# Moving the regroupings of k and q behind the additions to ut, in a fused sigmoid-attention and MLP-mixer kernel

## The chip, the cores and the metric

The kernel runs on one core of one Trainium2 chip. The metric is the device time of one execution in microseconds, and the number quoted for a kernel is the median of its timed executions. Besides those there is one profiled execution, whose trace gives each engine's instructions in order of time. Engines are named as the profile names them: PE is the matrix engine (PEld its weight loads), DVE the vector engine, ACT the scalar engine, POOL the GpSimd engine, SP the engine that here only issues DMAs.

## The reference

Inputs q, k and v have the shape (8 batches, 12 heads, 448 positions, 64). Attention without a softmax is followed by a mixer over positions (token part) and over channels (channel part):

```
scores = q @ k^T / 8 - log(448);  x = sigmoid(scores) @ v     # x: (8, 448, 768)
h  = relu(x^T @ w_tok1) @ w_tok2;  u  = x + h^T               # 448 -> 256 -> 448
h2 = relu(u @ w_ch1) @ w_ch2;      out = u + h2               # 768 -> 1536 -> 768
```

## The kernel before, in words

**Cycles.** The work runs in 24 cycles, three per batch: batch b, unit u (0, 1, 2), cycle c = 3b + u. A unit is four of the twelve heads. The instruction order of every engine is written out by hand; nothing is scheduled by a planner, and each engine executes its own list in order. In cycle c, PE computes the scores of (b, u) in seven pieces (`qk`, L184), between them the attention output of the unit before (`av`, tile `xa`, L211), the token part of the unit two cycles back (`tok_tail`, `tok1`, tile `tk`, then `ytrans`, tile `yt`, L312), and pieces of the channel part of an earlier batch (`c` tiles; L367 and L605 are the second channel product, L491 the first one, done once per batch behind the third cycle in the function `sevens`, in a scheme with seven block products).

**What DVE does in a cycle.** It casts `xa` out of PSUM (`xT`, L220, with a small copy L226), adds the token part to it (`ut`, L319, "the additions to ut"), adds and moves out the channel results (`o`, L564, L571, L757), and regroups the loaded k and q (L126): `raw_k` and `raw_q` hold a batch as it was loaded, `rel_k` and `rel_q` the same with pairs of heads side by side. Three regroupings, one per unit, make one tensor of one batch.

**PSUM banks.** `xa`, `tk` and `yt` of batches from the third on take turns in banks 0 and 1: the next user on PE waits until DVE or ACT has read the one before. So PE's `xa` of a cycle waits for the additions to ut of the cycle before, and PE's `tk` waits for the casts `xT`.

**SP's queue.** SP issues, in order, the DMA transposes of k and q of the coming batch (`tr_k`, `tr_q`, L139, 21 blocks of 128x128 each), of the attention output (`xn`, L236, 8 blocks), of the sum u (`un`, L326, 24 blocks), and the stores of the results (L577, L766). A transpose of k or q is issued when its three regroupings are done. `tr_k` and `tr_q` of a batch are read by the first `qk` of that batch.

**POOL's queue.** After the opening, POOL only issues loads. `gated_loads(b)` first copies two columns of `tr_q` of batch b+1 (L971, "the gate"), so that it waits for that transpose, and then issues the loads of v of batch b+1 and of k and q of batch b+2, each in two halves. There is one buffer for the loaded k and one for q, and two for v.

**Where the regroupings stand.** `through_dma(b, 0)` is the list of eight pieces "regroup k three times, transpose k, regroup q three times, transpose q":

```
for t in ("k", "q"):
    for u in range(u0, NU):
        pieces.append(lambda t=t, u=u: relayout(b, t, u))
    pieces.append(lambda t=t: dma_transpose(b, t, u0))
```

Cycles 6 to 8 (third batch) hand the pieces for the fourth batch out one at a time between pieces of channel work (`work`), and `sevens` takes up to two that are left. Cycles 9 to 23 call `some(n)` at two places: n = `within` after the third `qk`, n = `behind` at the end of the cycle, ahead of `ytrans`.

Of the kernel before, what the change touches and what calls it, by code (L numbers as in the profile page):

```python
# [23 lines left out]
NU = 3  # L24
# [6 lines left out]
def kernel(  # L31
# [13 lines left out]
    B, H, S, E = q.shape  # L45
# [39 lines left out]
    def bank(shape, dtype, name):  # L85

        if opening_banks:
            n = opening_banks.pop(0)
        else:
            n = at_bank[0]  # L90
            at_bank[0] = (n + 1) % 4
        return pp.tile(shape, dtype, tag=f"m{n}", bufs=1, name=name)
# [7 lines left out]
    def raw_tile(b, t):  # L100
        if (b, t) not in raw:
            tag, bufs = f"raw_{t}", 2 if t == "v" else 1
            if b == 1 and t != "v":
                tag = f"rel_{t}"
            raw[b, t] = pa.tile(
                [128, NU, 2, NJ, E], FP16, tag=tag, bufs=bufs, name=f"raw_{t}_{b}"
            )
        return raw[b, t]

    def load(b, t, src, u0, u1):  # L110

        for g in range(2):
            dst = raw_tile(b, t)[64 * g : 64 * g + 64, u0:u1, :, :, :]
            heads = src[b, 6 * g + 2 * u0 : 6 * g + 2 * u1]
            nc.gpsimd.dma_start(
                out=dst.rearrange("p u hi j e -> p (u hi) (j e)"),
                in_=heads.rearrange("h (p j) e -> p h (j e)", j=NJ),
            )

    def relayout(b, t, u):  # L120

        if (b, t) not in rel:
            rel[b, t] = pa.tile(
                [128, NU, NJ, 2, E], FP16, tag=f"rel_{t}", bufs=1, name=f"rel_{t}_{b}"
            )
        nc.vector.tensor_copy(  # L126
            out=rel[b, t][:, u, :, :, :],
            in_=raw[b, t][:, u, :, :, :].rearrange("p hi j e -> p j hi e"),
        )
# [8 lines left out]
    def dma_transpose(b, t, u0, u1=NU):  # L138
        nc.sync.dma_start_transpose(  # L139
            out=tr_tile(b, t)[:, u0:u1, :, :].rearrange("e u j r -> e (u j) r"),  # L140
            in_=rel[b, t][:, u0:u1, :, :, :].rearrange("r u j hi e -> r (u j hi e)"),
        )

    def through_dma(b, u0):

        pieces = []
# [4 lines that stand above are left out]
        return pieces  # L151

    def by_unit(b, u0):

        pieces = []
# [4 lines that stand above are left out]
                pieces.append(lambda t=t, u=u: dma_transpose(b, t, u, u + 1))  # L160
        return pieces
# [143 lines left out]
    def ytrans(b, u, banks=()):  # L305
        for g in range(2):
            db = NU * g + u
            if banks:
                at_bank[0] = banks[g]
            ps = bank([128, 512], FP32, f"yt_{b}_{db}")  # L310
            for tcb in range(2):
                nc.tensor.matmul(  # L312
                    out=ps[:, 0:S],
                    lhsT=h1[b, u][:, tcb, g, :],
                    rhs=w2[:, tcb, :, :],
                    start=(tcb == 0),
                    stop=(tcb == 1),
                )
            nc.vector.tensor_tensor(  # L319
                out=uts[b % 2][:, db, 0:S], in0=xTs[b % 2][:, u, g, 0:S], in1=ps[:, 0:S], op=ADD  # L320
            )
# [531 lines left out]
    def pieces_ch2(b, groups):  # L853
        for t, half in groups:
            for n in range(0, NCB, 3):
                yield 3 * DH, lambda t=t, half=half, n=n: ch2(b, t, half, n, n + 3)

    def pieces_last(b):
        for n in range(0, NCB, 3):
            yield 3 * DH, lambda n=n: ch2_last(b, n, n + 3)  # L860
# [108 lines left out]
    def gated_loads(b):  # L969

        nc.gpsimd.tensor_copy(  # L971
            out=gate[:, :], in_=tr[b + 1, "q"][:, NU - 1, NJ - 1, 126:128]
        )
        if b > 1:
            load(b + 1, "v", v, 0, NU)
        for t, src in (("k", k), ("q", q)):
            if b + 2 < B:
                load(b + 2, t, src, 0, NU)

    ON_DMA = range(N_FIRST, N_CYCLES)  # L980

# [3 lines left out]
    for c, cb in ((N_FIRST, 3), (N_FIRST + 1, 8)):  # L985
        b, u = divmod(c, NU)
        before = divmod(c - 1, NU)
        ahead = divmod(c + 1, NU)
        copies = []
# [27 lines left out]
        if u == 2:  # L1017
            copies = by_unit(2, 1)
# [33 lines left out]
    pending, copies = [], []  # L1052
    early = weight_sums()
    lane = [0]
    for c in range(2 * NU, ONE_RUN):
        b, u = divmod(c, NU)
        before, ahead = divmod(c - 1, NU), divmod(c - 2, NU)


        if c == 2 * NU:  # L1060
            first = c
            pending, shares = [*pieces_ch2(0, by_half[2:]), *pieces_last(0)], [10, 10, 10]
            total = sum(w for w, f in pending)
            spent = 0

        def work(share):
            goal = 3 * sum(shares[: c - first]) + share * shares[c - first]
            done = 0
            while pending and spent + done < total * goal / 90:
                w, f = pending.pop(0)  # L1070
                if len(pending) % 4 == 3:
                    lane[0] ^= 1
                at_bank[0] = 2 + lane[0]
                f()
                done += w
                if copies:
                    copies.pop(0)()
                elif early:
                    early.pop(0)()
            return done  # L1080

        qk(b, u, 0)
        qk(b, u, 1)
        at_bank[0] = 0
        av(*before)
        xtrans_dma(*before)
        qk(b, u, 2)
        if c == 2 * NU + 2:
            copies += through_dma(3, 0)[NU + 1 :]
        spent += work(1)  # L1090
        qk(b, u, 3)
        qk(b, u, 4)
        at_bank[0] = 0
        tok_tail(*ahead)
        tok1(*ahead, with_scores=True)
        if c == 2 * NU + 1:
            copies = through_dma(3, 0)[: NU + 1]
        spent += work(2)
        if c == 2 * NU + 2:
            utrans(b - 1)  # L1100
            token_sums(b - 1)
        qk(b, u, 5)
        qk(b, u, 6)
        if u < 2:
            at_bank[0] = 0
            ytrans(*ahead)
        spent += work(3)
        if u == 2:
            sevens(b - 1)
            at_bank[0] = 0  # L1110
            ytrans(*ahead)
            gated_loads(b)
    assert not copies and not pending and not early

    def some(n):
        for f in copies[:n]:
            f()
        del copies[:n]

    for c in range(ONE_RUN, N_CYCLES):  # L1120
        b, u = divmod(c, NU)
        before, ahead = divmod(c - 1, NU), divmod(c - 2, NU)
        if b == NU:
            within, behind = ((0, 0), (4, 2), (2, 0))[u]
        else:
            within, behind = 2, 2
        if u == 0:
            assert not copies
            copies += through_dma(b + 1, 0) if b + 1 < B else output_sums()

        X, Y = 2, 0
        at_bank[0] = X
        turn0, turn1, rest = ch2_pair(b - 2, u)
        part = len(turn1) * 2 // 3
        qk(b, u, 0)
        qk(b, u, 1)
        for f in turn0:
            f()  # L1140
        qk(b, u, 2)
        some(within)
        if c == ONE_RUN + 2:
            gated_loads(b)
        if u == 2:
            utrans(b - 1)
        at_bank[0] = Y
        av(*before, 0, 4)
        qk(b, u, 3)
        av(*before, 4, NJ)  # L1150
        xtrans_dma(*before)
        if u == 2:
            token_sums(b - 1)
        qk(b, u, 4)
        for f in turn1[:part]:
            f()
        qk(b, u, 5)
        for f in turn1[part:]:
            f()
        at_bank[0] = Y  # L1160
        tok_tail(*ahead)
        qk(b, u, 6)
        tok1(*ahead, with_scores=True)
        rest()
        some(behind)
        if u == 1 and NU < b < B - 1:
            gated_loads(b)
        if u == 2:
            at_bank[0] = Y + 1
            for w, f in pieces_last(b - 2):  # L1170
                f()
            sevens(b - 1)
        at_bank[0] = Y
        ytrans(*ahead)
    assert not copies


# [5 lines left out]
    def halves(b, t, half):  # L1183
        return [lambda n=n: ch2(b, t, half, n, n + 6) for n in (0, 6)]

    first, second = halves(lot, 2, 0), halves(lot, 2, 1)
# [33 lines left out]
    first, second = halves(B - 1, 2, 0), halves(B - 1, 2, 1)  # L1220
# [47 lines left out]
```

## Time and profile before

| | us |
|---|---|
| median of three timed executions | 348.65 (347.54, 348.65, 351.4) |
| the profiled execution, its own time | 347.11 |
| its span, from the first to the last instruction | 345.3 |
| PE busy | 338.2 (98%) |
| DVE busy | 213.7 (62%) |
| ACT busy | 210.9 (61%) |
| POOL busy | 56.7 (16%) |
| three regroupings of a tensor (L126, about 0.61 each) | 1.67 to 1.8 |

The busy time of PE is modelled from pipelined matrix products, so that a short wait inside a run of products shows as a longer run, and not as idle time. In the lines of the timeline, the first number is the start in us from the span's beginning, the second the length, and the brackets behind a line tell how long the engine sat idle before it and what ended that. The DMA of a transpose or a load goes on after the issuing engine is done with it; the trace gives the time "to landing" apart.

### The profile page before, as it was taken

The page shows a single profiled execution, that of the slowest core. Times are in us where ns is not written, and L with a number is a line of the kernel's source. Part 1 is how long each engine was busy: PE and PEld are TensorE (multiplying, and loading weights), DVE is VectorE, ACT ScalarE, POOL GpSimd, SP SyncE. Part 2 cuts the span into 40 slices and gives each one's busy share as a digit, 9 for nine tenths or more (in the row PEclk, how much of TensorE's full clock was granted, in tenths as well). Part 3 has the DMA queues.
Part 4 walks back from the last instruction along what each step waited for, and adds up shares of the span by engine and source line. Part 5 has one row for each costly group of instructions (what it writes and reads, how often), then busy time and mean ns, then how long its engine had stood idle before and what let it go on. Part 6 is the DMA issues. An engine that isn't in the chain of part 4 may idle for free.

```text
span 345.3 us, 10256 instructions
## 1 busy us (share of the span) xinstructions
PE 338.2 (98%) x4465; PEld 241.5 (70%) x4465; DVE 213.7 (62%) x427; ACT 210.9 (61%) x271; POOL 56.7 (16%) x98
## 2 busy tenths in 40 slices
PE   7999999999999999999999999999999999999994
PEld 4555556555886679766896669766896779767962
DVE  2377466577775665756575654765665684976662
ACT  3996846487748865788448865688448875111400
POOL 8982440230040013000400013000100000000000
PEclk9999999999999999999999999999999999999999
DMA  7999999999999999989997999979963592035406
GB/s 120 174 170 189 208 203 203 169 175 219 200 181 205 198 184 208 153 126 164 181 228 87 165 193 156 199 108 170 176 135 30 82 171 68 1 78 128 79 2 159
DMA packets 104380, 52.17 MB, mean 151 GB/s; under 512 B 76432, under 2 KB 101264, under 8 KB 104336
## 3 DMA queue, kind: packets, MB, share of 16 engines
q1 hardware_dynamic: 78944, 29.70, 49.2%
q0 software_dynamic: 25168, 21.50, 41.5%
q8 instruction: 35, 0.57, 0.7%
q10 hardware_dynamic: 224, 0.33, 0.4%
q14 instruction: 9, 0.07, 0.1%
HBM read 43.45 MB, written 11.01 MB: 158 GB/s over the span
## 4 chain that ended last, share of the span: by engine, by line
PE 88%; ACT 4%; DMA 3%; DVE 2%; issue 1%; POOL 0%; DVEq 0%; ACTq 0%
PE c_ab L491 14%; PE c L367 12%; PE qk L184 9%; PE c_c L491 8%; PE xa L211 8%; PE c L605 6%; PE tk L289 5%; PE c L734 5%; PE yt L312 5%; PE c L541 4%; ACT att L191 4%; PE c L695 4%; PE c L344 3%; DMA raw_k<-in_k_dram 2%; DMA first_q<-in_q_dram 1%; PE c_b L491 1%
## 5 line engine op out<-in xcount | busy, mean ns | idle before, releaser
L191 ACT ACTIVATE att<-qk,att_bias 128x896 f16<-128x896 f32 x168 | 155.3, 1015 | 34.0 <-PE qk L184 33.7
L184 PE MATMUL qk<-tr_q,tr_k 64*64 64x448 f16 x672 | 59.5, 359 | 0.3 <-ACT att L191 0.2
L491 PEld LDWEIGHTS <-c 128*128 128x128 f16 x504 | 47.8, 98 | 1.9 <-issue 1.8
L367 PE MATMUL c<-c,h 64*64 64x384 f16 x960 | 47.1, 322 | 0.0
L220 DVE CAST xT<-xa 128x448 f16<-128x448 f32 x48 | 27.7, 620 | 31.1 <-PE xa L211 31.0
L211 PE MATMUL xa<-att,raw_v 64*64 64x448 f16 x672 | 40.3, 349 | 0.1
L512 ACT ACTIVATE pt_ab<-c_ab 128x896 f32<-128x896 f32 x21 | 19.3, 917 | 30.8 <-PE c_ab L491 30.8
L367 PEld LDWEIGHTS <-h 64*64 64x64 f16 x960 | 29.5, 107 | 11.0
L491 PEld LDWEIGHTS <-sum 128*128 128x128 f16 x378 | 36.3, 98 | 0.0
L184 PEld LDWEIGHTS <-tr_k 64*64 64x64 f16 x672 | 21.5, 105 | 19.2 <-issue 11.9
L564 DVE TENSOR_TENSOR o<-un,c 128x384 f32<-128x384 f16 x34 | 18.8, 554 | 23.9 <-PE c L605 20.6
L319 DVE TENSOR_TENSOR ut<-xT,yt 128x448 f16<-128x448 f16 x48 | 27.5, 614 | 2.5 <-PE yt L312 2.5
L211 PEld LDWEIGHTS <-raw_v 64*64 64x64 f16 x672 | 21.5, 107 | 10.6 <-issue 1.0
L971 POOL COPY gate<-tr_q 128x2 f16<-128x2 f16 x6 | 1.1, 184 | 153.0 <-DMA tr_q<-rel_q 153.0
L303 ACT ACTIVATE h<-tk 128x256 f16<-128x256 f32 x42 | 14.3, 412 | 14.8 <-PE tk L289 14.8
L541 PE MATMUL c<-c,h 128*128 128x384 f16 x120 | 22.3, 326 | 0.0
L312 PE MATMUL yt<-w,h 128*128 128x448 f16 x96 | 22.1, 353 | 0.0
L605 PE MATMUL c<-c,h 128*128 128x384 f16 x120 | 22.0, 326 | 0.0
L514 ACT ACTIVATE h<-c_ab 128x896 f16<-128x896 f32 x7 | 6.4, 917 | 24.4 <-PE c_ab L491 24.4
L289 PE MATMUL tk<-xn,w 128*128 128x256 f16 x156 | 21.2, 274 | 0.1
L521 DVE TENSOR_TENSOR h<-pt_c,c_c 128x448 f16<-128x448 f32 x21 | 13.0, 617 | 13.2 <-PE c_c L491 13.2
L521 DVE TENSOR_TENSOR h<-pt_ab,c_ab 128x896 f16<-128x896 f32 x14 | 15.2, 1084 | 9.6 <-PE c_ab L491 9.6
(100 smaller groups left out, 461.4 us busy)
## 6 DMA issues: line engine op xcount, KB each, us to landing
out_dram<-o SPq DMA_DIRECT2D x48, 192.0 KB, 2.9
c<-in_moe_w_ch_dram POOLq DMA_DIRECT2D x4, 1152.0 KB, 15.9
raw_k<-in_k_dram POOLq DMA_DIRECT2D x10, 336.0 KB, 10.8
raw_q<-in_q_dram POOLq DMA_DIRECT2D x10, 336.0 KB, 13.7
raw_v<-in_v_dram POOLq DMA_DIRECT2D x10, 336.0 KB, 8.0
out_dram<-o SPq DMA_DIRECT2D x15, 96.0 KB, 6.9
raw_q<-in_q_dram POOLq DMA_DIRECT2D x12, 112.0 KB, 5.0
raw_k<-in_k_dram POOLq DMA_DIRECT2D x12, 112.0 KB, 4.8
```

Of the source, the lines that this page charges most:

```text
L184: nc.tensor.matmul(out=ps[64 * g : 64 * g + 64, hi, 0:S], lhsT=tr[b, "k"][64 * hi : 64 * hi + 64, u, j, 64 * g : 64 * g + 64], rhs=tr[b, " ...
L191: nc.scalar.activation(out=att[b, u, j][:, :, :], in_=ps[:, :, 0:S], func=SIGMOID, bias=bias_t[:, :], scale=att_scale,)
L211: nc.tensor.matmul(out=ps[g][64 * hi : 64 * hi + 64, 0:S], lhsT=raw[b, "v"][64 * g : 64 * g + 64, u, hi, j, :], rhs=att[b, u, j][64 * g : ...
L220: nc.vector.tensor_copy(out=xTs[b % 2][:, u, g, 0:S], in_=ps[g][:, 0:S])
L289: nc.tensor.matmul(out=ps[tcb], lhsT=w1[rows, t, cols], rhs=xn[b, u][rows, :, t, :], start=(t == 0 and not with_scores), stop=(t == (2 if ...
L312: nc.tensor.matmul(out=ps[:, 0:S], lhsT=h1[b, u][:, tcb, g, :], rhs=w2[:, tcb, :, :], start=(tcb == 0), stop=(tcb == 1),)
L319: nc.vector.tensor_tensor(out=uts[b % 2][:, db, 0:S], in0=xTs[b % 2][:, u, g, 0:S], in1=ps[:, 0:S], op=ADD)
L367: nc.tensor.matmul(out=ps[p][m : m + 64, 0:n], lhsT=lhsT(p, part, m), rhs=rhs(p, part), start=(first and turn == 0), stop=(last and turn = ...
L491: nc.tensor.matmul(out=ps[:, g, p, :], lhsT=weights[n][:, d, 128 * cb : 128 * cb + 128], rhs=moving[n][:, d, :], start=(n in (1, 5, 2) and ...
L521: nc.vector.tensor_tensor(out=shaped(dst), in0=shaped(parts[gs, which]), in1=ps, op=ADD)
L541: nc.tensor.matmul(out=ps[:, 0:DH], lhsT=h2[b][:, BY_GROUP[cb], 128 * t : 128 * t + 128], rhs=c2[:, BY_GROUP[cb], cols], start=(cb == 0), ...
L605: nc.tensor.matmul(out=ps[p][:, 0:DH], lhsT=h2[b][:, BY_GROUP[n], 128 * t : 128 * t + 128], rhs=c2[:, BY_GROUP[n], DH * p : DH * p + DH], ...
```

## The change

Five edits in the order of instructions; no operation is added or left out.

1. In cycle 7 the list for the fourth batch's k is filled later: behind `ytrans`, ahead of the third share of channel work, and no longer behind `tok1`, ahead of the second share. Whatever is left of it runs on into cycle 8.
2. In cycles 9 to 23 `some(behind)` stands behind `ytrans`, hence behind the additions to ut, and no longer ahead of it (in the third cycle of a batch, behind `sevens` too).
3. In batches 4, 5 and 6 (counted from 0) the eight pieces are shared out differently: two regroupings of k at the end of the first cycle, the third and the transpose of k within the second, all of q at the end of the second.
4. `gated_loads` at the end of the second cycle moves along, behind `ytrans` and `some(behind)`.
5. From batch 3 on, `gated_loads` issues k, v, q, and no longer v, k, q. The call of batch 2 keeps v, k, q.

```diff
-        if b > 1:
+        first, second = b == 2, b > 2
+        if first:
             load(b + 1, "v", v, 0, NU)
-        for t, src in (("k", k), ("q", q)):
-            if b + 2 < B:
-                load(b + 2, t, src, 0, NU)
+        if b + 2 < B:
+            load(b + 2, "k", k, 0, NU)
+        if second:
+            load(b + 1, "v", v, 0, NU)
+        if b + 2 < B:
+            load(b + 2, "q", q, 0, NU)
...
         tok1(*ahead, with_scores=True)
-        if c == 2 * NU + 1:
-            copies = through_dma(3, 0)[: NU + 1]
         spent += work(2)
...
         if u < 2:
             at_bank[0] = 0
             ytrans(*ahead)
+        if c == 2 * NU + 1:
+            copies += through_dma(3, 0)[: NU + 1]
         spent += work(3)
...
-            within, behind = 2, 2
+            within, behind = ((0, 2), (2, 4), (0, 0))[u] if b < B - 1 else (2, 2)
...
         rest()
-        some(behind)
-        if u == 1 and NU < b < B - 1:
-            gated_loads(b)
         if u == 2:
...
             sevens(b - 1)
         at_bank[0] = Y
         ytrans(*ahead)
+        some(behind)
+        if u == 1 and NU < b < B - 1:
+            gated_loads(b)
```

Set side by side, the instruction lists of PE and ACT are the same in both kernels. DVE's, SP's and POOL's differ in order only. SP's list differs in one place, at the end of the third batch:

```
before: stores o_1, tr_k, xn, stores o_2, tr_q, un, stores o_3
after:  stores o_1, xn, stores o_2, tr_k, un, stores o_3, tr_q
```

## Prediction

> **What bounds the kernel now.** I read the page's head first, then PE's waits, then a table of stretches, then the timeline where stretches of the same work differ.
>
> ```profile
> span 345.3 us, 10256 instructions
> PE 338.2 (98%) x4465; PEld 241.5 (70%) x4465; DVE 213.7 (62%) x427; ACT 210.9 (61%) x271; POOL 56.7 (16%) x98
> ...
> PE qk L184 <- ACT att L191: 0.2, 1, 0.2
> ...
> 117.80:128.39 10.59, 10.59 (x168) 6.87 (x166) 7.51 (x15) 7.05 (x9) 0.18 (x1) 1.00 1.09 161
> ...
> 148.87:157.17 8.30, 8.30 (x144) 5.29 (x142) 5.11 (x10) 6.95 (x9) 0.00 (x0) 1.00 0.93 156
> 157.17:167.54 10.37, 10.37 (x168) 6.47 (x166) 6.46 (x13) 6.95 (x9) 1.77 (x4) 1.00 1.00 172
> ```
>
> PE is the bound: busy 98%, and behind the opening its only listed wait is 0.2 us. In the last three lines (stretch, length, busy time of PE, PEld, DVE, ACT, POOL, then clock and DMA) every ordinary cycle takes 8.30 us and every third cycle 10.37, full of PE work. Hence DVE's order can win only where a stretch is longer than its sisters: cycle 11 (10.59 for 10.37), cycles 22 and 23 (8.40 and 10.47), and cycle 8, which the timeline shows:
>
> ```profile
> 72.79 1.49 PE L211 MATMUL xa<-att,raw_v 64*64 64x448 f16 x28
> ...
> 78.61 1.15 DVE L126 COPY rel_k<-raw_k 128x896 f16<-128x896 f16 x2 [1.51 <-DMA raw_k<-in_k_dram]
> ...
> 80.66 1.14 DVE L319 TENSOR_TENSOR ut<-xT,yt 128x448 f16<-128x448 f16 x2
> ...
> 81.39 1.98 PE L211 MATMUL xa<-att,raw_v 64*64 64x448 f16 x28
> ```
>
> DVE stood idle 1.51 us for the load of k, regrouped it ahead of the additions to ut, and these ended at 81.80. PE's 28 products of xa took 1.98 us there, 1.49 in the cycle before: 0.49 us lost on the bank.
>
> **What the change wins.** *Cycle 8:* DVE now does weight sums (L409, 0.55 each) where it waited, o_1 at about 78.8, and the two additions end at about 80.95, ahead of 81.39. Gain 0.49. *Cycle 11:* today two regroupings (1.14) stand ahead of ut, and 16 products of xa take 1.12 us for 0.93; gain 0.2. *Cycles 22 and 23:* two sums of weights (1.02) stand ahead of ut, and xa runs 0.08 longer in each; gain 0.2 together. Sum 0.9 us. *Batches 4 to 6:* nothing to win, since their cycles are already 8.30 and 10.37.
>
> **What it may cost there.** In cycle 13 today ut ends at 159.35; three regroupings of q behind it (1.8) end near 160.5 (one fewer stands ahead), and the next xT starts at 161.47 after 2.12 us of idle time. Behind the first cycle the two regroupings of k and the third, in a row, end at about 152.1, as today, and xT comes at 153.17. So xT hides both; cost 0 (without that cover, each 0.1 us past it would cost 0.1 in each of up to six cycles). The q transpose moves by 1.5 us, from 159.0, and is read at 180.4; un and xn behind it on SP have over 15 us too. Loads k, v, q: v is issued 1.3 us later, plus the 1.5, and may land as k does today (180.4); it is read in cycle 16, past 190. Cost 0. Were v 10 us later still, PE would wait.
>
> **Where something becomes late: the end of the third batch.** SP and POOL today:
>
> ```profile
> 81.47 5.38 SPq L139 DMA_TRANSPOSE tr_k<-rel_k  x1
> 86.95 1.25 SPq L236 DMA_TRANSPOSE xn<-xT  x1
> 88.29 1.19 SPq L577 DMA_DIRECT2D out_dram<-o  x2
> 89.58 4.80 SPq L139 DMA_TRANSPOSE tr_q<-rel_q  x1
> 94.42 3.74 SPq L326 DMA_TRANSPOSE un<-ut  x1
> 98.26 1.20 SPq L766 DMA_DIRECT2D out_dram<-o  x2
> ...
> 96.49 0.18 POOL L971 COPY gate<-tr_q 128x2 f16<-128x2 f16 x1 [22.02 <-DMA tr_q<-rel_q]
> ...
> 101.91 0.57 PE L184 MATMUL qk<-tr_q,tr_k 64*64 64x448 f16 x8
> ```
>
> The q transpose is issued at 89.58, lands at 96.49, and PE reads it at 101.91: 5.4 us to spare. In the new order SP does tr_k after the stores of o_2, and un and the stores of o_3 before tr_q. Step by step: xT of cycle 8 ends near 84.1 (84.6 less 0.49); xn 1.25 and the stores 1.2 from there, so tr_k starts at 86.7. The other issues of tr_k behind stores take 3.75 to 4.37 (mean 4.05), those of un behind a transpose 3.63 to 4.42 (mean 4.0), the stores 1.2, gaps 0.3. So tr_q is issued at 96.25. From issue to gate the five large transposes of q before took 6.91, 7.04, 6.51, 7.28 and 6.21 (mean 6.8): it lands at 103.05. PE, 0.49 earlier, is there at 101.42. PE waits 1.6 us, and the first cycle of the fourth batch is 1.1 later than today. Bounds: with the shortest rows (3.24, 3.63, 6.2) it lands at 101.3 and nothing waits; with the longest (5.38, 4.42, 7.3) at 105.3, 3.4 late. I take the means.
>
> The Trainium skill ("DMA: Bandwidth & Descriptors", section "Latency and other measured facts") gives DMA transposes an effective 261 GB/s. By that, the 0.69 MB of one tensor would move in 2.6 us, an estimate from that page, and tr_q would come in time; the trace has 6.2 to 7.3 us from issue to landing and disagrees, and the trace decides.
>
> **The second lateness, through the gate.** The loads of v, then k, then q wait for that landing, now 6.6 us later than 96.49. Cycle 10 regroups this k ahead of its xT:
>
> ```profile
> 111.09 1.67 DVE L126 COPY rel_k<-raw_k 128x896 f16<-128x896 f16 x3
> ...
> 113.82 1.16 DVE L220 CAST xT<-xa 128x448 f16<-128x448 f32 x2 [1.06 <-PE xa L211]
> ...
> 115.29 0.28 PE L270 MATMUL tk<-xn,w 64*64 64x256 f16 x4
> ```
>
> Today the halves of k are issued at 98.3 and 99.0 and take 10.4 to 9.5 us: landed at 108.7, 12.2 us behind the gate, 2.4 before it is wanted. In later batches the same distance is 13.7, 14.9 and 16.3; the shortest for a second tensor is that of q in batch 1, 10.6. In the new order un and the o_3 stores are no longer beside these loads, so I take 11.4, between the two nearest rows, 10.6 and 12.2. Then k lands at 114.45, regrouping ends at 116.1, xT (1.16 plus 0.1) at 117.4, where PE's tk products stood at 115.3: the cycle is 2.1 us later than today. That contains the 1.1 (the waits follow one another; the later one decides). Bounds: gate 101.3 and 10.6 give nothing late; gate 105.3 and 13.7 give 6.6. A neighbour of the same size: xn of cycle 9 was issued at 106.97 and landed 8.2 later, at 115.2, just ahead of tk at 115.29; 1.1 later with loads beside it, it is late by 1.0 to 1.1, and with the longest row (10.9) by 3.7. Behind this q lands near 119 and is regrouped past 120: nothing more.
>
> **Sum.** Later by 2.1 (it already holds the 0.49 of cycle 8), less 0.2 for cycle 11, less 0.2 for cycles 22 and 23: 1.7 us slower. Against the profiled execution, 347.11 = 345.3 of span and 1.8 around it, that makes 348.8. That execution stands 1.5 below the median of the timed ones, 348.65; the middle of all four is 348.1, and 348.1 + 1.7 gives 349.8. A measurement of this kernel can't tell less than about 1% (3.5 us) from no change, and this forecast lies inside that.
>
> **Rivals.**
> 1. *Nothing is late* (0.22): tr_q lands by 101.4 and k by 112.4. For it: the shortest rows, and no loads run beside the three transposes. Against it: three long DMAs in a row on one queue, each with rows that need the means. Then only the gains are left: 347.2, to 348.5 with half a microsecond of waiting.
> 2. *The fourth batch's loads come clearly late* (0.14), the other side: k lands 13.3 us or more behind a gate at 103, DVE holds xT behind it, PE waits for xT in cycle 10. It decides from a landing of k at 116.3 on, where the delay passes 3.9 and the net 3.5. For it: 13.7 to 16.3 in batches 3 to 5. Against: 12.2 in this batch. Time 351.6 to 354.3.
> 3. *A wait cools PE* (0.05). The opening's 16 warm-up products took 3.60 us, 225 ns each, four of the same at 10.31 only 0.61, 152 each: PE starts slow after standing still. If the wait in cycle 9 is at its bound of 3.4 late and PE then restarts as slowly, 16 products lose 1.2 us once more: 348.1 + 3.4 + 1.2 - 0.4 = 352.3, and more if it comes twice. No wait in the middle of this trace reaches 1 us, so it can't show that. The Trainium skill ("TensorE: Matmul & The Clock Gate", section "Part 1: The HAM clock gate") puts the threshold at an idle window of about 3.4 us; my waits of 1 to 2 lie below it.
> 4. *The change does less than it says* (0.06): DVE finds other idle time, tr_q overtakes nothing, and the time is as before, 348.1.
>
> The forecast itself (349.8, from 348.6 to 351.6) has 0.53. The range from the gains alone (347.2) up into rival 2 (353.0) leaves out what is above and below, about 2 in 10. **Chances:** faster by over 1% 0.04 (0.9 us can't do it, only the spread of executions), within 1% 0.78, slower 0.18 (rivals 2 and 3).
>
> **What would show it.** In the new trace: xa of cycle 8 back at 1.49; tr_q issued near 96 and the gate near 103; a hole or a long qk at 101.4 to 103; DVE idle ahead of rel_k in cycle 10 with DMA raw_k as its releaser; cycles of batches 4 to 6 at 8.30 and 10.37 as now. I am wrong if batches 4 to 6 change at all, or if the three transposes pack closer than 4 us.

## The result and the profile after

| | before | after |
|---|---|---|
| median of 22 timed executions, us | 347.79 | 351.24 |
| the profiled execution, us | 347.11 | 349.38 |
| its span, us | 345.3 | 347.6 |

The ratio after to before is 1.0097, with a 95% interval of [1.0075, 1.0119]: slower by 3.4 us, twice the 1.7 of the forecast, inside its range, and just inside 1%. The profiled execution shows 2.3 of these 3.4 us; what the others add comes up below.

First the head of the page, PE's waits, and three stretches that answer to cycles 11, 13 and 14 (stretch, length, busy time of PE, PEld, DVE, ACT, POOL, then clock and DMA):

```profile
span 347.6 us, 10251 instructions
PE 337.7 (97%) x4465; PEld 239.4 (69%) x4465; DVE 213.3 (61%) x427; ACT 210.7 (61%) x271; POOL 57.1 (16%) x98
...
PE tk L270 <- DMA xn<-xT: 2.2, 1, 2.2
...
PE qk L184 <- DMA tr_q<-rel_q: 0.5, 1, 0.5
...
120.51:130.90 10.39, 10.39 (x168) 6.47 (x166) 7.50 (x15) 6.95 (x9) 0.04 (x1) 1.00 1.10 159
151.38:159.68 8.30, 8.30 (x144) 5.29 (x142) 5.11 (x10) 6.95 (x9) 0.00 (x0) 1.00 0.72 132
159.68:170.05 10.37, 10.37 (x168) 6.47 (x166) 7.51 (x15) 6.95 (x9) 0.86 (x3) 1.00 0.92 170
```

The later batches are as they were: 8.30 and 10.37. Cycle 11 fell from 10.59 to 10.39. Two new waits of PE stand in the list, both on DMA transposes. The timeline of the places that the prediction worked out:

```profile
79.97 1.15 DVE L319 TENSOR_TENSOR ut<-xT,yt 128x448 f16<-128x448 f16 x2
...
81.62 1.49 PE L211 MATMUL xa<-att,raw_v 64*64 64x448 f16 x28
...
87.16 4.08 SPq L139 DMA_TRANSPOSE tr_k<-rel_k  x1
91.28 4.27 SPq L326 DMA_TRANSPOSE un<-ut  x1
95.65 1.18 SPq L766 DMA_DIRECT2D out_dram<-o  x2
96.88 3.40 SPq L139 DMA_TRANSPOSE tr_q<-rel_q  x1
...
102.17 0.19 POOL L971 COPY gate<-tr_q 128x2 f16<-128x2 f16 x1 [28.50 <-DMA tr_q<-rel_q]
...
102.18 0.57 PE L184 MATMUL qk<-tr_q,tr_k 64*64 64x448 f16 x8 [0.46 <-DMA tr_q<-rel_q]
...
107.46 1.35 SPq L236 DMA_TRANSPOSE xn<-xT  x1
...
113.45 1.67 DVE L126 COPY rel_k<-raw_k 128x896 f16<-128x896 f16 x3 [2.00 <-issue]
115.04 1.15 DVE L220 CAST xT<-xa 128x448 f16<-128x448 f32 x2
...
117.98 0.30 PE L270 MATMUL tk<-xn,w 64*64 64x256 f16 x4 [2.25 <-DMA xn<-xT]
```

The stall of cycle 8 is gone (xa 1.49). The transpose of q is issued at 96.88 and opens the gate at 102.17, 5.7 us later than before; PE waits 0.46 for it. In cycle 10 DVE stands idle 2.0 us ahead of the regrouping of k. The profile names no DMA there (`issue`), but k's second half, issued at 104.6, took 8.8 us at most, and 113.4 is where the regrouping begins. DVE is done with xT at 116.2. PE still waits until 117.98, for xn, which was issued at 107.46 and took 10.5 us to land, where it took 8.2 before. From the views by tile, k, q and xn after (first issue to last issue, then the time to landing):

```profile
L115 POOL DMA_DIRECT2D raw_k<-in_k_dram x2: 687/692/697, 104.0 to 104.6; - x2
DMA to landing us min/median/max: 6.5/7.6/8.8
...
L115 POOL DMA_DIRECT2D raw_q<-in_q_dram x2: 672/674/677, 106.0 to 106.7; - x2
DMA to landing us min/median/max: 9.3/10.1/10.9
...
L236 SPq DMA_TRANSPOSE xn<-xT x1: 1349/1349/1349, 107.5 to 107.5; - x1
DMA to landing us min/median/max: 10.5/10.5/10.5
```

and q and xn before (the 8.2 is that of the xn issued at 107.0):

```profile
L115 POOL DMA_DIRECT2D raw_q<-in_q_dram x2: 669/672/675, 100.4 to 101.0; - x2
DMA to landing us min/median/max: 10.7/12.0/13.4
...
L236 SPq DMA_TRANSPOSE xn<-xT x2: 1241/1252/1264, 107.0 to 116.7; - x2
DMA to landing us min/median/max: 4.0/6.1/8.2
```

The starts of `yt` (L312), the last work of each cycle on PE, cut the profile into cycles. From one start to the next, in us:

| ending with | before | after | difference |
|---|---|---|---|
| cycle 8 (with `sevens`) | 21.90 | 21.42 | -0.48 |
| cycle 9 | 8.30 | 8.83 | +0.53 |
| cycle 10 | 8.30 | 10.74 | +2.44 |
| cycle 11 (with `sevens`) | 22.75 | 22.56 | -0.19 |
| cycles 12 to 21 | 8.30, 8.30, 22.55 in turn | the same | within 0.02 |
| cycles 22 and 23 | 8.38, 22.64 | 8.30, 22.55 | -0.17 |

With 0.22 us that arose ahead of cycle 7, where nothing was changed, these make the 2.34 us by which the last `yt` stands later (314.13 for 311.79).

**What the profiled execution doesn't show.** Of the 22 timed executions of the changed kernel, 15 have a mean granted clock of 0.995 or less, and their median is 351.5; the other seven, at 0.997 or more like the profiled one, have 349.9. Of the 86 executions of the kernel before that were timed beside the experiments, seven are at 0.995 or less. So PE's clock has a part in the loss; the second and the seventh experiment look at that.

### The profile page after: what moved, and what is told of

Read it like the earlier page. It is cut to its first block, busy times and chain, and to the rows that moved or that the text cites. A ratio compares the mean times of both kernels' runs of the same rounds, so it can differ in the third digit from the quotient of the medians.

```text
span 347.6 us, 10251 instructions
## 1 busy us (share of the span) xinstructions
PE 337.7 (97%) x4465; PEld 239.4 (69%) x4465; DVE 213.3 (61%) x427; ACT 210.7 (61%) x271; POOL 57.1 (16%) x98
## 4 chain that ended last, share of the span: by engine, by line
PE 86%; DMA 6%; ACT 4%; DVE 1%; issue 1%; SPq 0%; DVEq 0%; ACTq 0%
PE c_ab L491 13%; PE c L367 11%; PE qk L184 9%; PE xa L211 8%; PE c_c L491 7%; PE c L541 6%; PE tk L289 5%; PE c L605 5%; PE c L734 5%; PE yt L312 5%; ACT att L191 4%; PE c L695 4%; DMA xn<-xT 3%; PE c L344 3%; DMA tr_q<-rel_q 1%; DMA first_q<-in_q_dram 1%
## 5 line engine op out<-in xcount | busy, mean ns | idle before, releaser
L184 PE MATMUL qk<-tr_q,tr_k 64*64 64x448 f16 x672 | 58.1, 359 | 0.8 <-DMA tr_q<-rel_q 0.5
L211 PE MATMUL xa<-att,raw_v 64*64 64x448 f16 x672 | 39.6, 349 | 0.0
L367 PEld LDWEIGHTS <-h 64*64 64x64 f16 x960 | 28.5, 107 | 11.5
L184 PEld LDWEIGHTS <-tr_k 64*64 64x64 f16 x672 | 20.6, 105 | 20.3 <-issue 12.7
L211 PEld LDWEIGHTS <-raw_v 64*64 64x64 f16 x672 | 20.4, 107 | 10.7 <-issue 0.3
L303 ACT ACTIVATE h<-tk 128x256 f16<-128x256 f32 x42 | 14.3, 413 | 14.8 <-PE tk L289 14.8
L312 PE MATMUL yt<-w,h 128*128 128x448 f16 x96 | 22.1, 353 | 0.0
L605 PE MATMUL c<-c,h 128*128 128x384 f16 x120 | 22.0, 326 | 0.0
```

The lines of the kernel that those rows point to most:

```text
L184: nc.tensor.matmul(out=ps[64 * g : 64 * g + 64, hi, 0:S], lhsT=tr[b, "k"][64 * hi : 64 * hi + 64, u, j, 64 * g : 64 * g + 64], rhs=tr[b, " ...
L211: nc.tensor.matmul(out=ps[g][64 * hi : 64 * hi + 64, 0:S], lhsT=raw[b, "v"][64 * g : 64 * g + 64, u, hi, j, :], rhs=att[b, u, j][64 * g : ...
L312: nc.tensor.matmul(out=ps[:, 0:S], lhsT=h1[b, u][:, tcb, g, :], rhs=w2[:, tcb, :, :], start=(tcb == 0), stop=(tcb == 1),)
L367: nc.tensor.matmul(out=ps[p][m : m + 64, 0:n], lhsT=lhsT(p, part, m), rhs=rhs(p, part), start=(first and turn == 0), stop=(last and turn = ...
L605: nc.tensor.matmul(out=ps[p][:, 0:DH], lhsT=h2[b][:, BY_GROUP[n], 128 * t : 128 * t + 128], rhs=c2[:, BY_GROUP[n], DH * p : DH * p + DH], ...
```

## The experiments

Medians are of 4 to 12 executions, each beside 17 to 29 of the kernel before on the same chip. "Cycles 8 to 11" are the four lengths of the table above, from the experiment's own profile.

### 1. Edit 1 undone

```diff
         tok1(*ahead, with_scores=True)
+        if c == 2 * NU + 1:
+            copies = through_dma(3, 0)[: NU + 1]
         spent += work(2)
...
-        if c == 2 * NU + 1:
-            copies += through_dma(3, 0)[: NU + 1]
         spent += work(3)
```

> The changed kernel with edit 1 undone (k of the fourth batch handed out from cycle 7's second share on, as before); edits 2 to 5 kept. Theory A (all of the loss comes from edit 1, through SP's order at the end of the third batch): the gate of the third batch is back near 96.5, no wait of PE in cycles 9 and 10, the gains in cycles 11, 22 and 23 stay (0.36 us), the gain of 0.48 in cycle 8 is lost: 0.4 us faster than before, ratio about 0.999. Theory B (the other edits carry the loss): still 2 to 3.5 us slower than before, ratio 1.006 to 1.010.

Measured: 346.94 for 347.73, ratio 0.9972 [0.9943, 1.0]. Cycles 8 to 11: 21.63, 8.30, 9.00, 22.55; the gate opens at 96.50, and the one new wait is 0.5 us for xn in cycle 10, where I expected none. Cycle 8 is 0.27 shorter than before, where I expected no gain. Theory B is out: in sum, edits 2 to 5 lose nothing that can be measured. One profile can't tell whether the longer cycle 10 comes from them or varies from execution to execution.

### 2. Edit 1 alone, in the kernel before

```diff
         tok1(*ahead, with_scores=True)
-        if c == 2 * NU + 1:
-            copies = through_dma(3, 0)[: NU + 1]
         spent += work(2)
...
+        if c == 2 * NU + 1:
+            copies += through_dma(3, 0)[: NU + 1]
         spent += work(3)
```

> The kernel before with edit 1 alone. Theory A: the whole loss, 2.3 to 3.8 us slower than before, ratio 1.007 to 1.011, with PE waiting 0.5 us for tr_q at 102 and 2 us or more for xn or k in cycle 10. Theory B: no loss, or the 0.5 us gain of cycle 8 alone, ratio 0.998 to 1.000.

Measured: 352.81 for 347.73, ratio 1.0125 [1.007, 1.018]. Edit 1 carries the whole loss. Cycles 8 to 11: 21.79, 8.96, 12.52, 22.79. Cycle 10 is 1.8 us longer than with the change, though its wait for xn (2.40) is nearly the same. The stretches of this experiment's profile show why (the column ahead of the last two is the granted clock):

```profile
116.00:118.00 2.00, 0.00 (x0) 0.00 (x0) 0.80 (x3) 0.56 (x1) 0.00 (x0) 1.00 1.15 274
118.00:120.00 2.00, 1.73 (x15) 1.07 (x16) 0.00 (x0) 1.12 (x2) 0.00 (x0) 0.74 1.25 246
120.00:122.00 2.00, 2.00 (x8) 0.93 (x7) 0.55 (x1) 0.44 (x2) 0.00 (x0) 0.50 1.74 194
122.00:124.00 2.00, 2.00 (x26) 1.04 (x28) 1.46 (x3) 0.31 (x1) 0.00 (x0) 0.91 0.32 66
```

and, in its timeline, the same eight products of L605 that take 1.46 us elsewhere:

```profile
118.27 0.30 PE L270 MATMUL tk<-xn,w 64*64 64x256 f16 x4 [2.40 <-DMA xn<-xT]
...
119.74 2.77 PE L605 MATMUL c<-c,h 128*128 128x384 f16 x8
```

After standing still for 2.4 us, PE is granted half its clock, from about 119.0 to 122.4: 0.26 + 0.50 + 0.09 of three 2 us stretches are 1.7 us of lost work. The clock of rival 3 of the prediction is here, at a wait shorter than I had asked for it and one cycle later.

### 3. un issued behind tr_q

```diff
         if c == 2 * NU + 2:
-            utrans(b - 1)
             token_sums(b - 1)
...
         spent += work(3)
         if u == 2:
+            utrans(b - 1)
             sevens(b - 1)
```

> The changed kernel with the un transpose of cycle 8 issued behind tr_q, so that SP does tr_k, stores o_3, tr_q, un. Theory A: tr_q is issued near 92.6, the gate opens near 98.5 (2 us later than before, 3.7 earlier than with the change), loads start then, xn lands in time or up to 0.5 late, no wait for tr_q: all gains (0.84) stay, 0.3 to 0.8 us faster than before, ratio 0.9975 to 0.9995. If un must not be late itself (read by o at 108.9), a new wait of DVE shows there; I expect it to land by 105. Theory B: as slow as the change, ratio 1.007 to 1.010.

Measured: 348.12 for 347.73, ratio 1.0008 [0.9977, 1.004], slower than I expected, though most of the loss is gone. Cycles 8 to 11: 21.42, 8.30, 10.66, 22.55. tr_q is issued at 93.76 and the gate opens at 99.26, so the wait for tr_q is gone; but xn, issued at 106.92, again lands only 10.6 us later, and PE waits 2.2 us for it in the profiled execution. The clock held there; in 3 of 12 executions it is at 0.995 or less. So xn doesn't simply follow the gate.

### 4. The gate on tr_k

```diff
         nc.gpsimd.tensor_copy(
-            out=gate[:, :], in_=tr[b + 1, "q"][:, NU - 1, NJ - 1, 126:128]
+            out=gate[:, :], in_=tr[b + 1, "k" if b == 2 else "q"][:, NU - 1, NJ - 1, 126:128]
         )
```

> The changed kernel, SP's order kept, but the gate of the third batch reads tr_k in place of tr_q, so that v, k and q load from about 94 on. Theory A with the gate as its link: xn and k come in time in cycle 10 and that wait (2.2 us and more) goes; but tr_q now moves beside the loads and lands 0 to 3 us later than 102, so that PE waits 0.5 to 3.5 us in cycle 9. Net between 0.3 faster and 2.5 slower than before, at least 0.8 us better than the change. If the lateness of tr_q itself, and not the gate, carried the loss, the time stays as with the change (3.4 slower).

Measured: 360.61 for 347.73, ratio 1.0366 [1.0324, 1.0408], a miss by far. Cycles 8 to 11: 21.42, 22.69, 8.30, 22.55. Cycle 10 is whole again, as expected, with v, k and q loading from 94.7 on. But tr_q, issued at 96.55 beside these loads, kept SP for 11.7 us:

```profile
96.55 11.70 SPq L139 DMA_TRANSPOSE tr_q<-rel_q  x1
...
113.00 0.96 PE L184 MATMUL qk<-tr_q,tr_k 64*64 64x448 f16 x8 [11.63 <-DMA tr_q<-rel_q]
```

It landed at 112.9, just behind the last load (98.1 + 13.2 = 111.3 at the earliest). PE stood still for 11.6 us and came back at half its clock. So this transpose, issued behind the loads of v and k and 1.5 us ahead of that of q, came through when they did. The gate that makes the loads wait for tr_q protects tr_q; xn has no such protection.

### 5. No wait for k ahead of xT

```diff
-            within, behind = ((0, 0), (4, 2), (2, 0))[u]
+            within, behind = ((0, 0), (0, 6), (2, 0))[u]
```

> The changed kernel with the three regroupings of k and its transpose in cycle 10 moved from within the cycle (ahead of xT) to its end. DVE then waits for no load ahead of xT. Theory X (PE's wait in cycle 10 is for xn, which moves through the DMA engines behind the three loads): the wait of 2.2 us for xn stays, the time is that of the change, ratio 1.007 to 1.012 against before. Theory K (it is DVE's wait for the load of k, my sum's decisive term): that wait falls away, 1.5 us or more better than the change, ratio 1.000 to 1.005.

Measured: 351.66 for 347.42, ratio 1.0112 [1.0065, 1.0159]. Cycles 8 to 11: 21.93, 8.81, 12.87, 22.73.

```profile
114.70 1.16 DVE L220 CAST xT<-xa 128x448 f16<-128x448 f32 x2 [2.64 <-PE xa L211]
...
119.37 0.43 PE L270 MATMUL tk<-xn,w 64*64 64x256 f16 x4 [3.04 <-DMA xn<-xT]
```

xT now comes as soon as PE has made xa, and PE waits for xn as before, 3.0 us here. Theory K, the decisive term of my sum, is out; theory X stands.

### 6, 8, 9, 10. Loads held back until xn has landed

The sixth kernel holds back k and q of the fifth batch:

```diff
+        if first:
+            return
         if b + 2 < B:
             load(b + 2, "k", k, 0, NU)
...
-            within, behind = ((0, 0), (4, 2), (2, 0))[u]
+            within, behind = ((0, 0), (0, 4), (4, 0))[u]
...
         some(behind)
+        if c == ONE_RUN:
+            nc.gpsimd.tensor_copy(out=gate[:, :], in_=xn[2, 2][:, 1, 3, 126:128])
+            load(4, "k", k, 0, NU)
+            load(4, "q", q, 0, NU)
```

> The changed kernel, in which the gate of the third batch lets only v load, and k and q of the fifth batch load behind the landing of xn of cycle 9; k is regrouped at the end of cycle 10, q within cycle 11. SP's order and the late tr_q stay. Theory X: xn, issued at 107.5, lands 3.1 to 5 us later (by 112.5, not 118), no wait in cycle 10; left are 0.5 us at tr_q and perhaps up to 0.6 us for q in cycle 11: 0.8 us faster to 0.6 slower than before, ratio 0.9977 to 1.0017, and the granted clock stays at 1.0 in that stretch. If xn is slow for another reason than these loads, it lands near 118 again and the ratio stays at 1.007 or above.

The eighth adds the edit of the third experiment:

> The two remedies together: un issued behind tr_q, and k and q of the fifth batch loaded behind xn. Theory A with X: no wait of PE at tr_q nor in cycle 10, all the gains of the change (0.84 us) are left, less up to 0.6 if q comes late in cycle 11: ratio 0.9975 to 0.9995 against before. Other theories: a wait is left that I don't know, ratio above 1.000.

The ninth is the third with q alone held back, and the regroupings where the change has them; the tenth is the first experiment with q alone held back:

```diff
-        if b + 2 < B:
+        if b + 2 < B and not first:
             load(b + 2, "q", q, 0, NU)
...
         some(behind)
+        if c == ONE_RUN:
+            nc.gpsimd.tensor_copy(out=gate[:, :], in_=xn[2, 2][:, 1, 3, 126:128])
+            load(4, "q", q, 0, NU)
```

> The changed kernel with un issued behind tr_q, and of the loads of the third batch's gate only q put behind the landing of xn of cycle 9; k and v load at the gate, and the regroupings stay where the change has them (k within cycle 10, q at its end). Theory A with X: the gate opens near 98.5, v and k land by 109 to 110.5, xn lands 3 to 5 us after its issue at 106.5 to 107, q lands by 117.5 ahead of its regrouping near 119.5. No wait of PE in cycles 9 to 11, granted clock 1.0, cycles 8.30, 8.30 and the third as in later batches: 0.84 us faster than before, ratio 0.996 to 0.999. If k still holds DVE past 111.9, up to 0.5 of it is lost.

> The changed kernel with edit 1 undone (as the first experiment) and q of the fifth batch loaded behind the landing of xn of cycle 9. Its profile should show cycle 10 at 8.30 without the 0.5 us for xn that the first experiment's profile had, and the gains of cycles 11, 22 and 23 (0.36): ratio 0.996 to 1.000 against before, equal to the first experiment within the measurement or up to 0.5 us better, and about 0.5 us slower than the run beside it, which also keeps the gain of cycle 8.

| run | ratio to before | cycles 8 to 11 |
|---|---|---|
| 6 | 1.0076 [1.0047, 1.0106] | 21.42, 8.91, 8.30, 27.11 |
| 8 | 1.0035 [1.0001, 1.0068] | 21.42, 8.30, 8.30, 24.57 |
| 9 | 1.0141 [1.0096, 1.0186] | 21.42, 8.30, 8.30, 27.51 |
| 10 | 0.9993 [0.9959, 1.0026] | 22.27, 8.30, 8.30, 23.63 |

All four repaired cycle 10: xn landed 4.5, 3.0, 6.0 and 3.3 us after its issue, and cycle 10 is 8.30 in each. But the time came back in cycle 11, and three of the four ratios lie above what I expected. From the ninth:

```profile
114.58 1.32 POOL L115 DMA_DIRECT2D raw_q<-in_q_dram  x2 [1.77 <-DVE xT L220]
...
123.94 1.67 DVE L126 COPY rel_q<-raw_q 128x896 f16<-128x896 f16 x3 [4.92 <-DMA raw_q<-in_q_dram]
...
126.19 0.95 PE L270 MATMUL tk<-xn,w 64*64 64x256 f16 x4 [2.89 <-DVE xT L220]
```

q, issued at 114.6 where it was 106.0 with the change and 103.1 in run 3, lands near 124, and DVE waits for it ahead of xT. In 6 and 9 PE's clock fell to 0.50 after that wait as well. The wait was moved, not taken away; in run 10 what is left of it on PE is 0.4 and 0.2 us.

Together with the others these runs bear on what sets the landing of xn (issue, and issue plus landing time, from each trace; "last load" is the first issue of the last tensor plus the longer landing of its halves, so the end may be up to 0.7 later):

| kernel | xn issued | last load landed | xn landed |
|---|---|---|---|
| before | 107.0 | q 113.8 | 115.2 |
| after | 107.5 | q 117.0 | 118.0 |
| 1 | 107.6 | q 112.8 | 116.6 |
| 2 | 107.6 | q 117.4 | 118.2 |
| 3 | 106.9 | q 116.5 | 117.5 |
| 5 | 108.1 | q 118.5 | 119.4 |
| 7 | 107.1 | q 117.2 | 118.0 |
| 11 | 106.8 | q 114.4 | 115.6 |
| 6 (v alone ahead) | 106.5 | v 109.4 | 111.0 |
| 8 (v alone ahead) | 106.3 | v 106.6 | 109.3 |
| 9 (v, k ahead) | 106.5 | k 110.9 | 112.5 |
| 10 (v, k ahead) | 108.1 | k 109.7 | 111.4 |

Issued within 2 us of each other, xn lands 0.8 to 1.7 us behind the last of the loads that were issued ahead of it. In run 8 the loads were nearly through and xn took 3.0 us, so run 10, where it took 3.3, hardly tests this. Run 1, with 3.8 us behind the last load, is the one row that doesn't fit, and it stays unexplained. The Trainium skill ("DMA: Bandwidth & Descriptors", section "Queues, rings and completion order") says that a DMA's semaphore increment lands only after every earlier write of the same DMA engine, across its queues; that agrees with the table, and the runs can't tell it from a plain shortage of the engines.

### 7. PE kept busy through the wait

```diff
+        if (b, u) == (2, 2):
+            for _ in range(20):
+                nc.tensor.matmul(
+                    out=tks[b][0],
+                    lhsT=ident[:, :],
+                    rhs=c1[:, 0, 0:256].rearrange("p (g d) -> p g d", g=2),
+                    start=True,
+                    stop=True,
+                )
         for tcb in range(2):
             part = slice(64 * tcb, 64 * tcb + 64)
```

> The changed kernel with 20 products of 128x256 (about 2.15 us) on PE ahead of the tk products of cycle 10, in their bank; they take the place of standing still, and the tk products overwrite what they leave. Theory C (part of the loss in the median execution is PE's clock, which falls to half after that wait; the wait itself is 2.2 to 2.4 us): the wait ends at the same time, the clock stays at 1.0, the median falls by 1 to 1.8 us against the change, ratio 1.004 to 1.007, and the granted clock of nearly all its executions is 0.997 or more, where with the change 15 of 22 were at 0.995 or less. Without a part of the clock: as the change, 1.009 to 1.011, or slower by what the products take beyond the wait.

Measured: 350.32 for 347.42, ratio 1.0086 [1.0052, 1.0119]. The clock did as theory C says: all 12 executions are at 0.997 or more, where 15 of 22 were below with the change. The time gained is smaller than I expected, and within the intervals it can't be told from none. The profile shows a reason: cycle 10 takes 11.50 us, 0.76 more than with the change at full clock (10.74), because the products began only when xT had left their bank and ended behind the landing of xn:

```profile
116.07 2.34 PE L269 MATMUL tk<-c,ident 128*128 128x256 f16 x20 [0.73 <-DVE xT L220]
```

So the clock falls because PE stands still. What that costs is best read from the change's own executions, 351.5 against 349.9, and from the four profiles in which it fell at a wait in cycle 10 or 11 (runs 2, 5, 6 and 9): read in stretches of 1 us, the clock is at 0.50 for about 3.4 us in each, 1.7 us of lost work each time.

### 11. The regroupings of k all at once

```diff
         if c == 2 * NU + 1:
-            copies += through_dma(3, 0)[: NU + 1]
+            for f in through_dma(3, 0)[: NU + 1]:
+                f()
```

> The changed kernel, in which the three regroupings of the fourth batch's k and its transpose come all at once in cycle 7, right behind the additions to ut, and not one by one between pieces of channel work. SP's order at the end of the third batch is then that of the kernel before (tr_k, xn, stores o_2, tr_q, un), and ut still stands ahead of k. Theory A: tr_k is issued near 83, tr_q near 89.5 as before, the gate opens near 96.5, no wait for tr_q, xa of cycle 8 at 1.49: all gains (0.84 us) are left, less up to 0.5 for xn in cycle 10, which had no slack before either: ratio 0.9965 to 0.9995 against before, granted clock 1.0. If only the later place of k itself, and not SP's order behind it, carried the loss, it stays above 1.005.

Measured: 347.15 for 347.95, ratio 0.9965 [0.9939, 0.9992]. Cycles 8 to 11: 21.68, 8.30, 8.89, 22.56. The loss of the change is gone, and the median lies 0.8 us below that of the kernel before.

```profile
82.62 4.36 SPq L139 DMA_TRANSPOSE tr_k<-rel_k  x1
87.08 1.25 SPq L236 DMA_TRANSPOSE xn<-xT  x1
88.42 1.18 SPq L577 DMA_DIRECT2D out_dram<-o  x2
89.70 5.00 SPq L139 DMA_TRANSPOSE tr_q<-rel_q  x1
...
96.75 0.18 POOL L971 COPY gate<-tr_q 128x2 f16<-128x2 f16 x1 [22.83 <-DMA tr_q<-rel_q]
...
81.47 1.49 PE L211 MATMUL xa<-att,raw_v 64*64 64x448 f16 x28
...
115.71 0.30 PE L270 MATMUL tk<-xn,w 64*64 64x256 f16 x4 [0.40 <-DMA xn<-xT]
```

k is regrouped behind the additions to ut, as the change wanted, but in one go between them and the next xT. SP's order stays that of the kernel before, the gate opens at 96.75, xa takes 1.49. What is left is 0.4 us for xn in cycle 10 and, in cycle 8, a wait of 0.44 of PE's weight loads for an earlier xn, so that the cycle gains 0.22 and not 0.48. Clock 0.997 or more in all 12 executions. It was not k's place behind the additions that cost the time, but SP's order behind it: tr_k late, and un and the stores of o_3 ahead of tr_q.

Whether this version also beats the kernel before is less sure. In its one profile gains and losses cancel, and the last `yt` stands at 311.86, for 311.79 before; the same holds for run 1, once the 0.87 us that arose ahead of cycle 7 are taken off. The 0.8 us rest on the medians alone, by an interval that ends just below 1.

## Why the prediction was right or wrong

**Right.** PE bounds the kernel and the later batches can't win: no cycle from 12 to 21 moved by more than 0.02. The gains came at their size: 0.48 in cycle 8 (forecast 0.49), 0.19 in cycle 11 (0.2), 0.17 in cycles 22 and 23 (0.2). The loss came where it was put, at the end of the third batch, by the path that was named: SP's new order, tr_q late, the gate late, the loads late, a wait in cycle 10. Experiments 1, 2 and 11 show that edit 1 carries it through SP's order, 3 and 4 what an earlier gate does, 5 and 6 which wait is the last.

**Off in size: tr_q.** It was issued at 96.88 (forecast 96.25), but the gate opened 5.3 us later and not 6.8: 102.17 for 103.05, a wait of 0.46 for 1.6. In the five kernels with un and the stores of o_3 ahead of tr_q (the change and runs 2, 5, 6 and 7) it is 5.3 to 5.4 us, below my lower bound of 6.2; where un is issued right behind it, 5.5 to 5.9 (runs 3, 8 and 9) and 6.2 to 7.3 (the five rows of before). No run shows which neighbour on SP makes the difference.

**Wrong: which wait ends last in cycle 10.** The step "k lands at 114.45, ... the cycle is 2.1 us later than today" got k's distance from the gate right (regrouping began 11.3 us behind it; I had taken 11.4), but with the gate 0.9 us earlier xT was done at 116.2. By an estimate, that alone would have cost some 0.7 us: PE stood idle from 115.73 (117.98 less 2.25), and the last copy of xT ended at 116.42. The neighbour decided: "late by 1.0 to 1.1" for xn rested on a landing of 8.2 us, though the text itself said that loads would now run beside it. It took 10.5. The runs show in its place that xn lands about a microsecond behind the last load, and that was to be had from the trace of before: q's load ended at 113.8, xn landed at 115.2, and tk stood at 115.29. A gate 5.7 us later, with loads that then need 14.8 us up to q's landing, gives the 118 that was measured.

**Wrong: the clock.** Rival 3 had 0.05 and asked for a wait of 3.4 us. That was for a wait in cycle 9, and with a loss of 1.2 us behind it; here a wait of 2.2 to 2.4 in cycle 10 (as the profiles show it) was enough in most executions, and the loss was 1.7. The sum for one execution at full clock was nearly right, 1.7 against 2.1 (2.34 less the 0.22 ahead of cycle 7), and partly by luck: cycles 8 to 10 came out 2.5 longer where I had 2.1, with 0.6 less at tr_q than forecast and xn in the place of k. The median is at 3.4 because two thirds of the executions also pay about 1.6 us at half clock. The range was wide enough for both, though nothing in the sum allowed for the clock; the mechanism of rival 2 (k) decided nothing.

## What to carry to other kernels

When a step is moved, follow every DMA that is issued behind it in the same queue, and every load that a landing sets free: here a gain of half a microsecond on DVE let two other DMAs overtake one on SP, and that one held the gate of three loads. In nearly all of these runs a DMA transpose that was issued into running loads landed about when these did. So what must not be late has to be issued ahead of them, or the loads gated behind it, and the loads so held back need slack of their own. Where PE is the bound, price a wait of about 2 us as the wait plus the time at half clock that can follow, 1.7 us here in most executions.

## What was not expected of the hardware

- A stand of 2.2 to 2.4 us halved PE's granted clock in some executions and not in others: with the change a wait of 2.25 left it at 1.00 in the profiled execution, while 15 of 22 timed ones were at 0.995 or less; waits of 2.40 (run 2) and 2.21 (run 6) were followed by 0.50, one of 1.30 (run 8) by 1.00. In runs 2, 5, 6 and 9 it stayed low for about 3.4 us each time. The wait isn't all: run 3, with 2.2 us in its profile, has 3 of 12 timed executions at 0.995 or less, and run 10, with no wait above 0.4 behind the opening, has 4 of 12; no run shows why. The Trainium skill ("TensorE: Matmul & The Clock Gate", section "Part 1: The HAM clock gate") gives an idle window of about 3.4 us, free-running; the measured waits are shorter, and the measurement decides.
- The same transpose of q took 3.4 us to issue and 5.3 to land with no loads in flight, and 11.7 and 16.3 us with the loads of v and k ahead of it and that of q issued 1.5 us behind (run 4).
